# Batch 0's keys in fp32 over the SP queue, pads first, p in three gated loads, refitted load times and a new written order

## The chip, the core and the metric

The kernel runs on one core of one Trainium2 chip. The metric is device time in microseconds (us) of one launch. The engines are TensorE (PE, with its weight loads PEld), VectorE (DVE), ScalarE (ACT), GpSimd (POOL) and SyncE (SP), each of which takes its own list of instructions in order and waits on semaphores for the others. DMAs are issued by SP, by ACT and by POOL; POOL's can change the type on the way (fp32 to bf16), SP's here do not.

## The reference

Inputs: q, k, v of 8 batches x 8 heads x 576 tokens x 64, p of 8 x 8 x 32 x 64, and two weight matrices, 512 x 2048 and 2048 x 512. The output is 4608 x 512, fp32.

```python
p_packed = sm_attn(p, k, v)          # softmax(p k^T / 8) v : 32 packed rows per head
out = sm_attn(q, p_packed, p_packed) # softmax(q p_packed^T / 8) p_packed
x = out.transpose(0, 2, 1, 3).reshape(4608, 512)
y = relu(x @ w_in)**2 @ w_out
```

## The kernel before, in words

Work goes batch by batch (b = 0 to 7), heads in two halves of four (qd = 0, 1). The packed rows are multiplied with w_in first: M = p_packed w_in (32 rows per head, 2048 columns), so that the second softmax's weights, times M, give the hidden layer at once. All PE work is bf16 into fp32 PSUM.

The steps of a batch have names that the kernel's planner uses, and which the text below uses too (lines of the profile in brackets):
- Tk, Tq: DVE transposes of keys and queries (L589, L586). P, PT: cast and transpose of p (L541, L544).
- S1 (PE, L606), MX (DVE row maximum, L609), EX (ACT exp, L612), E (PE transposes, L618), EC (copy out of PSUM by ACT or DVE), PV (PE, L629), RC and XN (DVE, L633, L636): the first softmax and the packed rows. XQ (DVE, L640), XM (PE, L643), XC (copy): two transposed forms of them.
- M.b.0 to 3 (PE, L653), with the casts MC to bf16 on ACT or DVE (L509, L511): packed rows times a quarter of w_in's columns each.
- S2.b.x (PE, L670), then on DVE SI, SM, SU, SS, SN, SO (L683, L686, L690, L696 and L697, L701, L707), with SE (ACT exp, L693) between SU and SS: the second softmax over two parts x of a batch's tokens (three in batch 0). SO writes the weights a2 in the layout that PE needs.
- F1.b.fb (PE, L717; F.b.x.j at L744 for batches 0 and 1, by parts): 128 hidden columns from M and a2. R (relu, L726 and L728; L752 and L754) takes them out of PSUM into one of five buffers r_b, and the square SQ or Q (L734, L736; L762, L764) writes gT and frees the buffer.
- F2.t.fb (PE, L770): 36 tiles t of 128 tokens, 16 matmuls each, gT times w_out. FC copies a tile to one of four o_sb buffers (L509, L511), ST stores it with four DMAs (L785). The last tile is split in two (FZ, L791).

F1.b needs all of SO.b and its quarter of MC.b; F2 tile t needs the squares of the batches that it touches (tiles 9 to 12 lie in batch 2, tile 13 in 2 and 3, tiles 14 to 17 in 3). M and a2 have two buffers, so batch b waits there for F1 of b - 2.

The order of each engine's list is fixed when the program is built. `Plan.forward` (line 70) is a list scheduler: every step has a price per engine, a level (10 b and up) plus an offset from `TABLE['o']`, and where ACT and DVE can both do it, a lean from `TABLE['l']`. At every moment the ready step of the lowest level plus offset is taken. `Plan.run` (line 199) then emits the steps in order of their planned starts. `fills` (line 213) puts dummy matmuls (`keep_clock`, L515) into planned gaps of PE before the first F2. On the chip no planned time is kept, only the order and the semaphores.

Loads are planned as two steps, an issue on POOL (SP for the first half of batch 0's keys) and a stay on "DMA", in the order that the string `ORDER` (line 217) writes: k, v and q of a batch, `x` and `y` the two parts of batch 0's queries, `a0` to `a3` the quarters of w_in (four loads each), `b0` to `b7` eighths of w_out. At most eight POOL loads are under way: the ninth waits for the first to land. `dma_k0` (line 563) brings the first half of batch 0's keys in fp32 to the unused gT over SP, and `k0_cast` (line 567) casts it, part on DVE, part on ACT. `p_load` (line 532) loads p of batch 0 over ACT and p of the other seven batches in one load (448 KB) over SP, held back by a one-element memset (`p_gate`, line 536) until MX.0.1. `setup2` (line 521) zeroes the pads of four v buffers on POOL, four memsets behind the second w_out load.

Of the kernel before, what the change touches and what calls it, by code (L numbers as in the profile page):

```python
# [8 lines left out]
ACT = mybir.ActivationFunctionType  # L9
ALU = mybir.AluOpType  # L10
AX = mybir.AxisListType
F32 = mybir.dt.float32
# [3 lines left out]
D = 64  # L16
# [25 lines left out]
class Plan:  # L42
# [156 lines left out]
    def run(self):  # L199
        out, T = self.forward()  # L200
        free = dict(self.base)
        end = min(p.start for p in out if p.name[:2] == "F2")
        for p in sorted(out, key=lambda p: p.start):
            e, us, fn = p.alts[p.alt]
            if e == "PE" and p.start < end:
                self.keep(self.fills(p.start - free.get(e, 0.0), p.start))
            free[e] = p.end
            u = [[b for b in range(24) if m >> b & 1] for m in p.unit or ()]
            if fn is not None:
                fn(*u)  # L210
        return T

    def fills(self, gap, t):
        return max(0, int((0.9 * gap - 0.3) / (0.2135 if t < self.warm else 0.109))) if gap > 0.7 else 0


ORDER = "k0 v0 x0 a0 y0 a1 a2 a3 b0 b1 k1 b2 b3 v1 b4 q1 b5 b6 b7 k2 v2 q2 k3 v3 q3 k4 v4 q4 k5 v5 q5 k6 v6 q6 k7 v7 q7"

TABLE = {'o': {'Lk.0.0i': 13.26, 'Lk.0.0': -22.5, 'LP.0': 0.67, 'Lk.0.1i': -185.35, 'Lk.0.1': -2.85, 'Lv.0.0i': 94.46,
# [209 lines left out]
def kernel_impl(tc, q, k, v, p, w_in, w_out, out):  # L429
# [24 lines left out]
    with ExitStack() as ctx:  # L454
# [81 lines left out]
        def p_gate():  # L536
            nc.vector.memset(p_f[1][:, :1], 0.0)
# [25 lines left out]
        def dma_k0(slot):  # L563
            kq_of["k", 0, 0] = kq_b[slot]
            nc.sync.dma_start(k0_f, kq_src("k", 0, 0))
# [491 lines left out]
```

## Time and profile before

| | |
|---|---|
| median of 3 runs | 254.42 us (254.21 to 255.92) |
| the profiled execution | 254.59 us, span 252.8 us |
| PE, DVE, ACT, POOL busy | 231.7, 185.0, 146.6, 53.5 us |
| DMA queues: POOL's, SP's | 18.19 MB, 10.30 MB |
| first useful matmul (S1 of batch 0) | 6.24 us |
| S1 of batch 1 | 37.02 us |
| last matmul ends | 247.7 us |

The page gives busy time for each engine, the span in 40 slices (a digit is tenths of busy time, 6.3 us a slice), groups of instructions by line with the mean time of one, and what ended the idle time before them. A stretch's table gives busy time of every engine between two times. A row of the timeline has start, length, engine, line, operation, output and inputs, count, and in brackets idle time with what ended it. PE's ends are modelled: a single F2 matmul is listed with 379 ns, but in a dense row they start 0.21 to 0.22 us apart.

### The profile page before, as it was taken

The numbers are of one execution on the slowest core, as the hardware profiler recorded it, in microseconds if no ns is written. First come the engines' busy times: TensorE is split into PE (matmuls) and PEld (weight loads), VectorE is DVE, ScalarE is ACT, GpSimd is POOL, SyncE is SP. The second block draws the span as 40 slices with busy tenths as digits, with TensorE's granted clock in tenths as the row PEclk, the third lists the DMA queues.
The fourth block names the chain that finished last, engine by engine and source line by source line (L and its number), as shares of the span: only waits on it lengthen the run. The fifth ranks groups of instructions, "written<-read, shape, count | busy, mean of one in ns | idle before, by whom it ended". The sixth has DMA issues, their size and how long they took to land.

```text
span 252.8 us, 5947 instructions
## 1 busy us (share of the span) xinstructions
PE 231.7 (92%) x2364; PEld 131.0 (52%) x2396; DVE 185.0 (73%) x355; ACT 146.6 (58%) x250; POOL 53.5 (21%) x94
## 2 busy tenths in 40 slices
PE   6567898899799999999999999999999999999991
PEld 4344674345454556466453366465544574476451
DVE  3357896898789899866299999967769786956110
ACT  3224795359468669677349589188555591388000
POOL 8559944443334432000000000000000000000001
PEclk9799999999999999999999999999999999999998
DMA  6999999999999999840211210110330311230232
GB/s 151 186 179 172 193 202 207 206 223 244 222 222 205 238 241 210 157 102 2 57 33 40 65 42 23 43 42 3 83 79 19 88 30 40 54 75 0 62 78 70
DMA packets 27147, 29.00 MB, mean 115 GB/s; under 512 B 5776, under 2 KB 18832, under 8 KB 27120
## 3 DMA queue, kind: packets, MB, share of 16 engines
q0 software_dynamic: 17888, 18.19, 43.8%
q1 hardware_dynamic: 8864, 10.30, 15.6%
q8 instruction: 19, 0.31, 0.5%
q10 hardware_dynamic: 368, 0.13, 0.2%
q14 instruction: 8, 0.07, 0.1%
HBM read 37.22 MB, written 9.44 MB: 185 GB/s over the span
## 4 chain that ended last, share of the span: by engine, by line
PE 65%; DMA 17%; DVE 6%; POOL 4%; ACT 2%; issue 2%; SPq 2%; DVEq 0%; POOLq 0%
PE pb L770 36%; PE ps L717 18%; DMA out_dram<-o_sb 4%; DMA kq_b<-in_q_dram 4%; DMA v_b<-in_v_dram 3%; DMA w_in_b<-in_moe_w_in_dram 3%; DMA kq_b<-in_k_dram 3%; PE ps L744 2%; PE ps L653 2%; SPq L785 2%; PE ps L670 2%; PE pb L791 1%; PE ps L770 1%; POOL w_in_b L578 1%; DVE o_sb L511 1%
## 5 line engine op out<-in xcount | busy, mean ns | idle before, releaser
L770 PE MATMUL pb<-w_out_b,gT 128*128 128x512 bf16 x482 | 119.2, 379 | 2.3 <-issue 1.1
L770 PEld LDWEIGHTS <-gT 128*128 128x128 bf16 x560 | 51.8, 98 | 58.5 <-issue 6.2
L717 PE MATMUL ps<-a,M 128*128 128x288 bf16 x384 | 54.9, 286 | 0.2
L726 ACT ACTIVATE r_b<-ps 128x576 bf16<-128x576 f32 x79 | 46.3, 664 | 9.5 <-PE ps L717 9.0
L717 PEld LDWEIGHTS <-M 128*128 128x128 bf16 x384 | 37.4, 98 | 13.5
L736 DVE TENSOR_TENSOR gT<-r_b 128x576 bf16<-128x576 bf16 x73 | 32.9, 455 | 13.7 <-ACT r_b L726 9.6
L785 POOL DMA_DIRECT2D out_dram<-o_sb x2 | 1.1, 532 | 148.6 <-ACT o_sb L509 148.6
L509 ACT COPY o_sb<-pb 128x512 f32<-128x512 f32 (+1 forms) x21 | 11.9, 565 | 32.9 <-PE pb L770 30.7
L509 ACT CAST M<-ps 128x1024 bf16<-128x1024 f32 (+1 forms) x27 | 23.6, 922 | 12.3 <-PE ps L653 9.4
L693 ACT ACTIVATE e<-s 128x512 bf16<-128x512 f32 (+3 forms) x17 | 11.2, 660 | 16.3 <-DVE s L690 16.3
L612 ACT ACTIVATE e<-ps,n 128x576 bf16<-128x576 f32 x16 | 11.8, 738 | 14.3 <-DVE n L609 13.8
L744 PE MATMUL ps<-a,M 128*128 128x256 bf16 (+3 forms) x160 | 18.3, 262 | 1.2 <-DVE a L707 1.2
L609 DVE TENSOR_REDUCE n<-ps 128x1 f32<-128x576 f32 x16 | 11.6, 748 | 7.8 <-PE ps L606 7.7
L744 PEld LDWEIGHTS <-M 128*128 128x128 bf16 x160 | 13.7, 98 | 5.8 <-DVE a L707 1.9
L752 ACT ACTIVATE r_b<-ps 128x512 bf16<-128x512 f32 (+2 forms) x23 | 14.1, 650 | 4.3 <-PE ps L744 3.8
L511 DVE COPY o_sb<-pb 128x512 f32<-128x512 f32 x13 | 8.8, 679 | 10.4 <-PE pb L770 7.2
L734 ACT ACTIVATE gT<-r_b 128x576 bf16<-128x576 bf16 x23 | 14.6, 679 | 0.1
L586 DVE STREAM_TRANSPOSE qT<-kq_b 128x576 f32<-128x576 f32 (+2 forms) x18 | 12.3, 689 | 2.7 <-DMA kq_b<-in_q_dram 2.7
L770 PE MATMUL ps<-w_out_b,gT 128*128 128x512 bf16 x46 | 12.2, 379 | 1.6 <-DVE o_sb L511 0.8
L589 DVE STREAM_TRANSPOSE kT<-kq_b 128x576 f32<-128x576 f32 x16 | 12.0, 754 | 2.2 <-DMA kq_b<-in_k_dram 2.2
L683 DVE STREAM_TRANSPOSE s<-ps 128x512 f32<-128x512 f32 (+3 forms) x17 | 12.1, 731 | 1.9 <-PE ps L670 1.7
L574 POOL DMA_DIRECT2D v_b<-in_v_dram x16 | 11.2, 708 | 9.7 <-DMA kq_b<-in_k_dram 3.6
(63 smaller groups left out, 258.4 us busy)
## 6 DMA issues: line engine op xcount, KB each, us to landing
out_dram<-o_sb SPq DMA_DIRECT2D x138, 64.0 KB, 2.0
kq_b<-in_k_dram POOLq DMA_DIRECT2D x15, 288.0 KB, 10.7
v_b<-in_v_dram POOLq DMA_DIRECT2D x8, 320.0 KB, 10.7
v_b<-in_v_dram POOLq DMA_DIRECT2D x8, 256.0 KB, 9.9
w_in_b<-in_moe_w_in_dram POOLq DMA_DIRECT2D x16, 128.0 KB, 6.6
w_out_b<-in_moe_w_out_dram POOLq DMA_DIRECT2D x8, 256.0 KB, 9.3
kq_b<-in_q_dram POOLq DMA_DIRECT2D x7, 288.0 KB, 11.1
kq_b<-in_q_dram POOLq DMA_DIRECT2D x14, 144.0 KB, 10.2
```

The lines of the kernel that those rows point to most:

```text
L509: nc.scalar.copy(dst, src)
L586: nc.vector.transpose(qT[:, qd].rearrange("p s x -> p (s x)").bitcast(F32)[:, w], kq_of["q", b, qd][:].bitcast(F32)[:, w])
L589: nc.vector.transpose(kT[:, qd].rearrange("p s x -> p (s x)").bitcast(F32).rearrange("p (x a j2) -> p j2 x a", a=32, j2=2), kq_of["k", b, ...
L612: nc.scalar.activation(e1[:, qd], ps1[b, qd], ACT.Exp, bias=n1[b % 2][:, qd:qd + 1], accum_out=d1[b % 2][:, qd:qd + 1])
L683: nc.vector.transpose(flat(s2, b, x).rearrange("p (q n) -> p q n", q=NQD), ps2[b, x])
L717: nc.tensor.matmul(t[:, c], lhsT=M[b % 2][:, qd, fb * FB:(fb + 1) * FB], rhs=a2[b % 2][:, qd, c * HALF:(c + 1) * HALF], start=(qd == 0), s ...
L726: nc.scalar.activation(dst, src, ACT.Relu)
L734: nc.scalar.activation(dst, r, ACT.Square)
L736: eng.tensor_tensor(out=dst, in0=r, in1=r, op=ALU.mult)
L744: nc.tensor.matmul(t[:, c, m * w:(m + 1) * w], lhsT=M[b % 2][:, qd, fb * FB:(fb + 1) * FB], rhs=a2[b % 2][:, qd, o:o + w], start=(qd == 0) ...
L752: nc.scalar.activation(dst, ph["h", b, x, j], ACT.Relu)
L770: nc.tensor.matmul(po[t], lhsT=gT[:, fb, n0:n0 + P], rhs=w_out_b[:, fb, :], start=(fb == 0), stop=(fb == NFB - 1))
```

## The change

1. Both halves of batch 0's keys come in fp32 over SP, into four rows of gT, each with a cast on DVE and one on ACT (`KHW = 2`). POOL no longer issues the second half.
2. The pad memsets of the v buffers go to the head of POOL's list, before the first v load.
3. p comes in three loads: batch 0 over ACT as before, batch 1 (64 KB) over SP behind MX.0.1, batches 2 to 7 (384 KB) over SP behind XQ.1.
4. In `ORDER` the keys of batch 1 move ahead of b0 and b1, its values ahead of b2 and b3, its queries ahead of b4.
5. The planner's load times are changed: 2.0 us after an issue and 0.9 after the stay, with other stays.
6. `fills` counts gap time before `warm` (4.9 us, before 6.6) at 0.2135 us a matmul and the rest at 0.109. The list has 86 dummy matmuls instead of 68.
7. `TABLE` is another one, all offsets and leans (805 and 555 of them). The order of nearly every engine's list changes from the start to the end; the amount of work in the matmuls of the kernel proper does not. DVE has 367 rows in its list instead of 356, ACT 228 instead of 239.

```diff
-                self.keep(self.fills(p.start - free.get(e, 0.0), p.start))
+                self.keep(self.fills(free.get(e, 0.0), p.start))
...
-    def fills(self, gap, t):
-        return max(0, int((0.9 * gap - 0.3) / (0.2135 if t < self.warm else 0.109))) if gap > 0.7 else 0
+    def fills(self, a, b):
+        if b - a < 0.7:
+            return 0
+        cold = max(0.0, min(b, self.warm) - a)
+        return int(cold / 0.2135 + max(0.0, 0.9 * (b - a - cold) - 0.3) / 0.109)
...
-ORDER = "k0 v0 x0 a0 y0 a1 a2 a3 b0 b1 k1 b2 b3 v1 b4 q1 b5 b6 b7 k2 v2 q2 k3 v3 q3 k4 v4 q4 k5 v5 q5 k6 v6 q6 k7 v7 q7"
+ORDER = ("k0 v0 x0 a0 y0 a1 a2 a3 k1 b0 b1 v1 b2 b3 q1 b4 b5 b6 b7 "
+         "k2 v2 q2 k3 v3 q3 k4 v4 q4 k5 v5 q5 k6 v6 q6 k7 v7 q7")
+
+KHW = 2
...
-        p_f = [consts.tile([P, n * D], F32, name=f"p_f{n}") for n in (2, 14)]
+        p_f = [consts.tile([P, n * D], F32, name=f"p_f{i}") for i, n in enumerate((2, 2, 12))]
...
-        def p_gate():
-            nc.vector.memset(p_f[1][:, :1], 0.0)
+        def p_gate(i):
+            nc.vector.memset(p_f[i][:, :1], 0.0)
...
-        k0_f = gT[:, 0:2, :].rearrange("p a b -> p (a b)").bitcast(F32)
+        k0_f = [gT[:, 2 * qd:2 * qd + 2, :].rearrange("p a b -> p (a b)").bitcast(F32) for qd in QDS]
...
-        def dma_k0(slot):
-            kq_of["k", 0, 0] = kq_b[slot]
-            nc.sync.dma_start(k0_f, kq_src("k", 0, 0))
+        def dma_k0(qd):
+            kq_of["k", 0, qd] = kq_b[qd]
+            nc.sync.dma_start(k0_f[qd], kq_src("k", 0, qd))
...
-            add(f"{name}i", [("POOL", issue, fn)], list(deps) + old, line="load", level=-200)
-            add(name, [("DMA", us, None)], [f"{name}i"], line="dma", lag=1.8, level=-200)
+            add(f"{name}i", [("POOL", issue, fn)], list(deps) + old, line="load", lag=2.0, level=-200)
+            add(name, [("DMA", us, None)], [f"{name}i"], line="dma", lag=0.9, level=-200)
...
+        if KHW > 1:
+            add("I2", [("POOL", 2.1, setup2)], line="load", level=-250)
...
-        add("G", [("DVE", 0.06, p_gate)], ["MX.0.1"], level=-99)
-        add("LP.1i", [("SP", 0.5, lambda: p_load(1, 1, B, nc.sync))], ["G"], level=-99)
+        for i, n, gate in ((1, 1, "MX.0.1"), (2, 6, "XQ.1")):
+            add(f"G.{i}", [("DVE", 0.06, lambda i=i: p_gate(i))], [gate], level=-99)
+            add(f"LP.{i}i", [("SP", 0.5, lambda i=i, b0=(0, 1, 2, B)[i], b1=(0, 1, 2, B)[i + 1]: p_load(i, b0, b1, nc.sync))], [f"G.{i}"], lag=1.0, level=-99)
...
-        plan.warm, plan.keep = 6.6, keep_clock
+        plan.warm, plan.keep = 4.9, keep_clock
```

In the changed program's lists, as built, PE goes through F2.7, F2.9, F2.10 and F2.12 before PV.3, and then through S1.4, XM.3, F2.11 with M.3 and S2.3 among it, E.4, S1.5, PV.4, E.5, S1.6, PV.5, XM.5, XM.4, S2.4, E.6, S1.7, PV.6, F1.3 with F2.13 among it, M.4. DVE's list around it reads, in order:

```
FC.12 XN.3 XQ.3 MX.4.1 Tk.5.0 MC.3.0 MX.4.0 Tk.5.1 SI.3.0 SM.3.0 SI.3.1 EC.4.0 SM.3.1 EC.4.1
Tk.6.0 SU.3.1 Tk.6.1 MX.5.0 SS.3.1 MX.5.1 SN.3.1 SU.3.0 SO.3.1 Tq.4.0 MX.6.0 MX.6.1 SS.3.0
Tk.7.0 Tk.7.1 Tq.4.1 SN.3.0 RC.5 SO.3.0 XN.5 RC.4 XQ.5 XN.4 XC.5 XQ.4 XC.4 SI.4.0 RC.6 Tq.5.0
SI.4.1 MX.7.0 SM.4.1 MX.7.1 Tq.5.1 EC.7.0 RC.7 SQ.3.0 EC.7.1 SQ.3.1 SQ.3.2 SU.4.1 ...
```

More of the change, by code (lines that the diff above doesn't have):

```diff
@@ L211, in run @@
         return T
-    def fills(self, gap, t):
-        return max(0, int((0.9 * gap - 0.3) / (0.2135 if t < self.warm else 0.109))) if gap > 0.7 else 0
-ORDER = "k0 v0 x0 a0 y0 a1 a2 a3 b0 b1 k1 b2 b3 v1 b4 q1 b5 b6 b7 k2 v2 q2 k3 v3 q3 k4 v4 q4 k5 v5 q5 k6 v6 q6 k7 v7 q7"
-TABLE = {'o': {'Lk.0.0i': 13.26, 'Lk.0.0': -22.5, 'LP.0': 0.67, 'Lk.0.1i': -185.35, 'Lk.0.1': -2.85, 'Lv.0.0i': 94.46,
[207 rows of a table removed]
+    def fills(self, a, b):
[6 more added lines that the diff above has]
+KHW = 2
+TABLE = {'o': {'Lk.0.0i': 114.0, 'Lk.0.1i': -41.03, 'Lk.0.0': 7.9, 'LP.0': 105.76, 'Lk.0.1': -41.22, 'I2': 113.03,
[207 rows of a table added]
 def kernel_impl(tc, q, k, v, p, w_in, w_out, out):
@@ L558, in dma_kq, with k0_cast @@
                 nc.gpsimd.dma_start(t[64 * g:64 * g + 64, w], kq_src(nm, b, qd)[64 - 64 * g:128 - 64 * g, w])
-        k0_f = gT[:, 0:2, :].rearrange("p a b -> p (a b)").bitcast(F32)
+        k0_f = [gT[:, 2 * qd:2 * qd + 2, :].rearrange("p a b -> p (a b)").bitcast(F32) for qd in QDS]
         K0 = 10 * D
-        def dma_k0(slot):
-            kq_of["k", 0, 0] = kq_b[slot]
-            nc.sync.dma_start(k0_f, kq_src("k", 0, 0))
-        def k0_cast(i, eng):
+        def dma_k0(qd):
+            kq_of["k", 0, qd] = kq_b[qd]
+            nc.sync.dma_start(k0_f[qd], kq_src("k", 0, qd))
+        def k0_cast(qd, i, eng):
             w = slice(0, K0) if i == 0 else slice(K0, JT * D)
-            cast(eng, kq_of["k", 0, 0][:, w], k0_f[:, w])
+            cast(eng, kq_of["k", 0, qd][:, w], k0_f[qd][:, w])
         def dma_v(b, i):
@@ L816, in load @@
             old = [issued[-8]] if len(issued) >= 8 else []
-            add(f"{name}i", [("POOL", issue, fn)], list(deps) + old, line="load", level=-200)
-            add(name, [("DMA", us, None)], [f"{name}i"], line="dma", lag=1.8, level=-200)
+            add(f"{name}i", [("POOL", issue, fn)], list(deps) + old, line="load", lag=2.0, level=-200)
+            add(name, [("DMA", us, None)], [f"{name}i"], line="dma", lag=0.9, level=-200)
             issued.append(name)
-        add("Lk.0.0i", [("SP", 0.45, lambda: dma_k0(0))], level=-300)
-        add("Lk.0.0", [("DMA", 1.36, None)], ["Lk.0.0i"], line="dma", lag=1.7, level=-300)
-        add("LP.0", [("DMA", 0.25, None)], line="dma", lag=1.7, level=-299)
+        for qd in range(KHW):
+            add(f"Lk.0.{qd}i", [("SP", 0.4, lambda qd=qd: dma_k0(qd))], lag=0.8, line="SPk", level=-300)
+        if KHW:
+            add("Lk.0.0", [("DMA", 2.0, None)], ["Lk.0.0i"], line="dma", lag=0.55, level=-300)
+        add("LP.0", [("DMA", 0.25, None)], line="dma", lag=0.8, level=-299)
+        if KHW > 1:
+            add("Lk.0.1", [("DMA", 1.8, None)], ["Lk.0.1i"], line="dma", lag=0.6, level=-300)
+        if KHW > 1:
+            add("I2", [("POOL", 2.1, setup2)], line="load", level=-250)
         for x in ORDER.split():
@@ L838, in kernel_impl @@
                     kq_free[slot] = f"T{nm}.{n}.{qd}" + (".y" if y else "")
-                    if x == "k0" and qd == 0:
+                    if x == "k0" and qd < KHW:
                         continue
                     for g in (0, 1) if nm == "q" and qd == 1 else (None,):
-                        load(f"L{nm}.{n}.{qd}{y}" + ("" if g is None else f".{g}"), (js[1] - js[0]) * 0.0755 * (1 if g is None else 0.5),
+                        load(f"L{nm}.{n}.{qd}{y}" + ("" if g is None else f".{g}"), (js[1] - js[0]) * 0.088 * (1 if g is None else 0.5),
                              lambda nm=nm, n=n, qd=qd, slot=slot, g=g, js=js: dma_kq(nm, n, qd, slot, g, js), 0.56, old)
@@ L845, in kernel_impl @@
                 for i in range(2):
-                    load(f"Lv.{n}.{i}", 1.33 + 0.3 * i, lambda n=n, i=i: dma_v(n, i), 0.7, [f"PV.{n - NV}"] if n >= NV else [])
+                    load(f"Lv.{n}.{i}", 1.15 + 0.55 * i, lambda n=n, i=i: dma_v(n, i), 0.7, [f"PV.{n - NV}"] if n >= NV else [])
             elif x[0] == "a":
@@ L849, in kernel_impl @@
                     for qd in QDS:
-                        load(f"LWI.{n}.{i}.{qd}", 0.62, lambda n=n, i=i, qd=qd: dma_w_in(n, i, qd), 0.6)
+                        load(f"LWI.{n}.{i}.{qd}", 0.665, lambda n=n, i=i, qd=qd: dma_w_in(n, i, qd), 0.6)
             else:
-                load(f"LWO.{n}", 1.26, lambda n=n: dma_w_out(n), 0.73)
-        add("G", [("DVE", 0.06, p_gate)], ["MX.0.1"], level=-99)
-        add("LP.1i", [("SP", 0.5, lambda: p_load(1, 1, B, nc.sync))], ["G"], level=-99)
-        add("LP.1", [("DMA", 1.0, None)], ["LP.1i"], lag=2.0, level=-99)
-        for i, (b0, b1) in ((0, (0, 1)), (1, (1, B))):
+                load(f"LWO.{n}", 1.42, lambda n=n: dma_w_out(n), 0.73)
+        for i, n, gate in ((1, 1, "MX.0.1"), (2, 6, "XQ.1")):
+            add(f"G.{i}", [("DVE", 0.06, lambda i=i: p_gate(i))], [gate], level=-99)
+            add(f"LP.{i}i", [("SP", 0.5, lambda i=i, b0=(0, 1, 2, B)[i], b1=(0, 1, 2, B)[i + 1]: p_load(i, b0, b1, nc.sync))], [f"G.{i}"], lag=1.0, level=-99)
+            add(f"LP.{i}", [("DMA", 0.32 * n, None)], [f"LP.{i}i"], lag=0.9, level=-99)
+        for i, (b0, b1) in enumerate(((0, 1), (1, 2), (2, B))):
             add(f"P.{i}", [("DVE", 0.07 + (b1 - b0) * 0.066, lambda i=i, b0=b0, b1=b1: p_cast(i, b0, b1))], [f"LP.{i}"], level=-9)
             add(f"PT.{i}", [("DVE", 0.07 + (b1 - b0) * 0.066, lambda b0=b0, b1=b1: p_tr(b0, b1))], [f"P.{i}"], level=-9)
-        add("KC.0", [("DVE", 0.42, lambda: k0_cast(0, V))], ["Lk.0.0"], level=-10)
-        add("KC.1", [("ACT", 0.48, lambda: k0_cast(1, A))], ["Lk.0.0"], level=-10)
+        for qd in range(KHW):
+            add(f"KC.{qd}.0", [("DVE", 0.4, lambda qd=qd: k0_cast(qd, 0, V))], [f"Lk.0.{qd}"], level=-10)
+            add(f"KC.{qd}.1", [("ACT", 0.5, lambda qd=qd: k0_cast(qd, 1, A))], [f"Lk.0.{qd}"], level=-10)
         def lasts(b):
@@ L885, in kernel_impl @@
                 add(f"Tk.{b}.{qd}", [("DVE", 0.69, lambda b=b, qd=qd: tr_k(b, qd))],
-                    ([f"Lk.{b}.{qd}"] if b or qd else ["KC.0", "KC.1"]) + ([f"S1.{b - 1}" if b > 1 else f"S1.0.{qd}"] if b else []), line="Tk", level=L)
-            pt = f"PT.{min(b, 1)}"
+                    ([f"Lk.{b}.{qd}"] if b or qd >= KHW else [f"KC.{qd}.0", f"KC.{qd}.1"]) + ([f"S1.{b - 1}" if b > 1 else f"S1.0.{qd}"] if b else []), line="Tk", level=L)
+            pt = f"PT.{min(b, 2)}"
             if b in SOLO:
@@ L983, in kernel_impl @@
                     add(f"ST.{t}", [("SP", 2.45, lambda t=t: store(t))], [f"FC.{t}"], free=[(f"FC.{t}", 0)], lag=2.0, level=L)
-                    add(f"SD.{t}", [("DMA", 0.5, None)], [f"ST.{t}"], level=L)
+                    add(f"SD.{t}", [("DMA", 0.42, None)], [f"ST.{t}"], level=L)
                 else:
@@ L1002, in kernel_impl @@
         add("I", [("POOL", 0.7, lambda: masks.make_identity(nc, ident[:]))], ["Lv.0.1i"], level=-250)
-        add("I2", [("POOL", 2.1, setup2)], ["LWO.1i"], level=-250)
+        if KHW < 2:
+            add("I2", [("POOL", 2.1, setup2)], ["LWO.1i"], level=-250)
         p_load(0, 0, 1, nc.scalar)
         setup()
-        plan.base.update(DVE=1.4, POOL=1.2, ACT=2.1, SP=0.7, DMA=1.2, PE=1.1)
+        plan.base.update(DVE=1.4, POOL=1.2, ACT=2.1, SP=0.7, DMA=1.6, PE=1.1)
         plan.table = TABLE
-        plan.warm, plan.keep = 6.6, keep_clock
+        plan.warm, plan.keep = 4.9, keep_clock
         kernel_impl.plan = plan
```

414 rows, old and new, of the table TABLE are left out of this document.

## The prediction

> **What bounds the kernel now.** I read the page's busy shares, then its 40 slices, then the busy table of chosen stretches, then the DVE groups by shape, and last the timeline of PE around batch 3. All of it is one execution: span 252.8 us, 254.59 us in all, so 1.8 us lie outside the span; the median of three runs is 254.42.
>
> ```profile
> span 252.8 us, 5947 instructions
> PE 231.7 (92%) x2364; PEld 131.0 (52%) x2396; DVE 185.0 (73%) x355; ACT 146.6 (58%) x250; POOL 53.5 (21%) x94
> ...
> PE   6567898899799999999999999999999999999991
> ...
> DVE  3357896898789899866299999967769786956110
> ```
>
> TensorE is full from slice 6 on. What can move is the start (0 to 31 us), any hole torn into the rest, and the 5.1 us after the last matmul.
>
> ```profile
> 37.02:108.94 71.92, 67.76 (x750) 36.15 (x761) 62.12 (x114) 46.90 (x80) 26.00 (x44) 1.00 1.16 214
> ...
> 108.94:247.72 138.78, 136.85 (x1289) 76.33 (x1307) 99.11 (x188) 81.47 (x137) 0.87 (x2) 1.00 0.19 47
> ```
>
> Columns: stretch, length, busy PE, PEld, DVE, ACT, POOL, granted clock, DMA. 37.02 is batch 1's S1, 108.94 batch 3's first F1 chunk. PE is nearly seamless because DVE, with as much as 62 of 72 us of work, is spread beside it. At 88.94 comes PV.3, at 108.94 F1.3.0: in those 20 us DVE makes batch 3's weights (SO.3) while PE runs F1.2 and F2 tiles.
>
> ```profile
> 88.94 0.48 PE L629 MATMUL ps<-v_b,e1T 128*32 128x64 bf16 x40 [0.33 <-ACT r_b L726]
> ...
> 108.94 1.27 PE L717 MATMUL ps<-a,M 128*128 128x288 bf16 x9
> ```
>
> The price list of DVE:
>
> ```profile
> L736 DVE TENSOR_TENSOR gT<-r_b 128x576 bf16<-128x576 bf16 x73 | 32.9, 455 | 13.7 <-ACT r_b L726 9.6
> L589 DVE STREAM_TRANSPOSE kT<-kq_b 128x576 f32<-128x576 f32 x16 | 12.0, 754 | 2.2 <-DMA kq_b<-in_k_dram 2.2
> ...
> L609 DVE TENSOR_REDUCE n<-ps 128x1 f32<-128x576 f32 x16 | 11.6, 748 | 7.8 <-PE ps L606 7.7
> L586 DVE STREAM_TRANSPOSE qT<-kq_b 128x576 f32<-128x576 f32 x14 | 10.4, 751 | 0.8 <-DMA kq_b<-in_q_dram 0.8
> ...
> L511 DVE CAST M<-ps 128x1024 bf16<-128x1024 f32 x7 | 8.4, 1203 | 2.4 <-PE ps L653 2.4
> ```
>
> Over all shapes count times mean is 202.4 us, the busy time 185.0: neighbours overlap by 17.4/355 = 0.05 us, which I take off each. For PE I use start-to-start times of dense timeline stretches: F2 0.217 us, F1 0.49 a chunk, M 0.26, S1 0.65, E 0.28, PV 0.45, an S2 half 0.36, XM 0.23.
>
> **The start.** Key half k0.1 leaves POOL's queue for SP's, in fp32. Removed: one POOL issue (0.68) and a landing at 8.4. SP's fp32 half k0.0 was issued at 0.75 and used at 4.62; behind it, at about 300 GB/s (the 2 to 4 us windows), the second lands near 6.6. Added: a cast on DVE (0.49, the row of the first half) and on ACT (0.62), both on the path: S1.0.1 starts about 8.9 instead of 9.21. The pads, 1.96 us of POOL at 25.26, go to the head: the first v load issues at 1.95 + 1.96 - 0.68 = 3.23. Cover: the second fp32 half keeps the DMA rings busy until then; without cover it costs 1.28.
>
> ```profile
> 8.00:9.00 1.00, 0.00 (x0) 0.00 (x0) 0.62 (x1) 0.00 (x0) 0.36 (x1) 0.91 1.39 201
> 9.00:10.00 1.00, 0.79 (x8) 0.30 (x11) 0.80 (x2) 0.16 (x1) 0.60 (x2) 0.50 1.36 190
> ```
>
> The clock fell to 0.50 after PE stood idle from 6.93 to 9.21, and S1.0.1 took 1.15 us, S1.0.0 0.69. Twelve new fills stand in that gap: 0.46 back there, about 0.3 in E.0.0. p's 448 KB, in flight from 11.2 to 18.9 beside query and w_in loads, become 64 KB; 384 KB move past 40 us. At the windows' 190 GB/s that is 2.0 us of stream, less about 0.4 for the wider key half, so w_in's third chunk, whose wait ended last (PE until 26.38), lands about 1.6 earlier. Two small p steps (0.17, 0.15) join DVE. Walking M.0.3 and the F pieces on, S1.1 starts near 32.9 with 11.1 us of useful matmul done; before, that much was done at 37.0 - 2.8 = 34.2. **Start: -1.3**, between +1.3 (pads uncovered, nothing else) and -3.0 (all p bytes and all cold clock).
>
> **Up to PV.3.** k1, v1, q1 move up by two, two and one w_out loads (1.4 us each by the landings that POOL waits on); q1's last half, awaited at 44.78, comes near 42. But between S2.1 and SO.1.1 DVE now also has the large p cast and transpose (0.48 + 0.50) and Tk.2.0, whose key lands about 50.5. SP's queue: the last p load stands ahead of all stores, its gate opens near 42, the first store came at 50.76: no wait. From S1.1 to F1.3.0 before, 67.0 us of listed matmul took 71.9, 5.0 lost; I leave 5.0 (bounds 2 and 8). The changed PE list has 67.8 us from S1.1 through PV.3: it ends at 32.9 + 67.8 + 5.0 = 105.7.
>
> **The new order around batch 3** decides. PE's list now runs F2.7, 9, 10 and 12 in a row (11 us from F2.7.13 on) *before* PV.3; DVE then has only copies, because the next thing in its list, XN.3, needs PV.3. After it, DVE's list is:
> - XN.3 to SO.3.0: 32 pieces, 20.7 us. Only 9.9 are batch 3's; 10.8 are keys, maxima, queries and copies of batches 4 to 7.
> - XN.5 to SO.4.0: 44 pieces, 23.0 us. Eight of F1.3's squares (3.2) stand among 19.7 of batches 4 to 7.
> - SQ.3.8 to SQ.3.15: 14 pieces, 7.9 us, with both MC.4 casts that F1.4.0 needs.
>
> That is 51.5 us in series. PE's list beside it, S1.4 to F2.13.15, holds 27.5 us, of which F2.11 and F2.13 are all the filler there is: F2.14 to F2.17 need F1.3, F1.3.0 needs SO.3.0, each later F1.3 chunk a relu slot (5) freed by those squares, F2.13.15 needs SQ.3.15. Walked piece by piece with ACT's steps, from PV.3's end: SO.3.0 +21.0; then XM.4, S2.4, E.6, S1.7, PV.6 stand in PE's queue; F1.3.0 +25.8, F1.3.3 +34.3, SO.4.0 +44.7, F2.13.15 +52.9. **Starved: 52.9 - 27.5 = +25.4**; bounds 15 (the 30.5 us of batches 4 to 7 a third cheaper than their rows) and 30 (F1.3 on one PSUM pair throughout, 1.3 us a chunk from +34.3).
>
> **The clock in it.** The walk leaves PE idle from +8.9 to +12.2 and +16.3 to +21.3, longer than the 2.3 us after which the clock halved; fills stop at the first F2. At half clock the 15.3 us of PE from F1.3.0 on need 30.6 where the walk gives 27.1: **+3** (bounds 0, all under DVE, and 8, with the first part's chain doubled too).
>
> The Trainium skill (TensorE: Matmul & The Clock Gate, What's actually happening) puts both changes at about 3.4 us, idle to throttle and busy to release; this trace throttled after 2.3, but released after about 3 (9.2 to 12.2), which agrees. By the page's idle figure only the second gap would throttle, and this term would be about 1, the total 280.
>
> **The rest.** S2.6.0 to the end is 111.6 us of listed matmul; before, 137.2 listed took 138.8, so 113. F1.5 has relu on DVE alone: two relus and a square, 1.8 us, against 1.63 of PE, six pairs, +1. Against before: +0.7.
>
> **Sum.** 105.7 + 52.9 + 3 + 113 + 1 = 275.6; after the last matmul 5.1; outside the span 1.8: 282.5, **282 us**. As differences: 254.6 - 1.3 + 25.4 + 3 + 0.7 = 282.4.
>
> **Rivals.**
> - *A smaller hole.* DVE's pieces are cheaper with little beside them: hole at 15, 2 instead of 5 lost before PV.3, no clock term: 254.6 - 1.3 - 3 + 15 + 0.7 = 266. For it: the means come from a busy trace. Against it: the same rows are as long in its quiet stretches (a key transpose took 0.72 to 0.78 everywhere).
> - *Half clock to the end of F1.3 and beyond*: clock term 8, hole 30: 292. For it: sparse PE at +8.9 to +34. Against it: dense PE releases it within 3 us.
> - *Not slower.* The hole is covered: front pieces of batches 4 to 7 run while PE has F2, so that 51.5 shrinks to PE's 27.5. Place: SO.3.0 before F1.3.0. Price: 254.6 - 1.3 + 0.7 = 254.0, or 252.3 at the start's bound. It decides only if DVE's 51.5 comes under 30. Against it: both engines take their lists in order, and XN.3 heads that list.
>
> **How the numbers follow.** Forecast 0.63 (own range 272 to 290), smaller hole 0.20, half clock 0.10, not slower 0.07. Range 263 to 293, leaving out the last case, the low edge of the second and the high one of the third. 1% (2.5 us) is about what a measurement of this kernel can tell: faster 0.03, same 0.04, slower 0.93.
>
> **What would show it.** Right: PE slices of 3 to 6 tenths from about 106 to 160 us with DVE at 9, PE waiting for L713 (SO) and L742 or L734 pieces, clock below 1 in that stretch; F1.3.0 some 26 us behind PV.3; clock 1.0 at 8 to 12 us; S1.1 near 33. Wrong: a full PE row there, or DVE idle inside the hole, which would make another engine or a store its cause.

## The result, and the profile after

After: 291.8 us (median; 289.9 to 293.7), before beside it 254.3. The ratio is 1.147, with a 95% interval of 1.136 to 1.158. The profiled execution took 290.9 us, span 289.1. The forecast was 282 us, range 263 to 293. Of the runs below, some executions were slower at a lower granted clock; the ratios leave those out.

The page of the changed kernel: the busy shares, and three rows of the 40 slices (7.2 us each, numbered from 1, tenths busy; the last row is the granted clock).

```profile
span 289.1 us, 6036 instructions
PE 251.6 (87%) x2414; PEld 138.2 (48%) x2414; DVE 189.1 (65%) x367; ACT 145.6 (50%) x243; POOL 52.4 (18%) x93
...
PE   8777889669888999944676979999999999999994
...
DVE  3569888479597860799798999958928115534300
...
PEclk9979999968999999995585999999999999999999
```

PE's busy time rose too, from 231.7 to 251.6 us, although its work is the same but for 18 dummy matmuls. Part of that is matmuls at a lower clock, and part is missing records: the trace before has 2364 matmuls beside 2396 weight loads, this one 2414 of both. The row has two dents where the row before was full: a small one at slices 8 and 9 (51 to 65 us), with the clock down to 6, and the large one at slices 18 to 24 (123 to 173 us), with the clock down to 5. In the large one DVE is at 7 to 9 tenths; in slice 16, ahead of PV.3, DVE is at 0. The stretches between the prediction's own landmarks (busy PE, PEld, DVE, ACT, POOL, clock, DMA): from batch 1's S1 to the end of PV.3, from there to batch 6's first S2, from there to the last matmul.

```profile
33.91:117.22 83.31, 73.72 (x716) 39.00 (x715) 57.82 (x106) 44.35 (x74) 25.36 (x43) 0.96 1.04 190
117.22:171.60 54.38, 38.14 (x599) 20.00 (x591) 50.52 (x99) 28.10 (x50) 1.05 (x2) 0.78 0.08 18
171.60:284.87 113.27, 113.07 (x785) 60.88 (x784) 59.10 (x112) 56.44 (x91) 0.79 (x2) 1.00 0.21 51
```

The second is the foreseen hole: PE busy for 38.1 of 54.4 us, DVE for 50.5. The third is as seamless as before. The first is the surprise: 83.3 us where the forecast had 72.8. PE's timeline says where most of that went:

```profile
53.30 2.75 PE L776 MATMUL pb<-w_out_b,gT 128*128 128x512 bf16 x12
59.47 0.41 PE L612 MATMUL ps<-kT,pT 32*32 32x512 bf16 x4 [3.41 <-DVE pT L550]
```

Batch 2's S1 waited 3.41 us for PT.2. DVE's timeline shows why, and the list of DMA issues how long the load took (KB, then us from issue to landing):

```profile
57.62 0.56 DVE L547 TENSOR_SCALAR p_b<-p_f 128x768 bf16<-128x768 f32 x1 [3.64 <-DMA p_f<-in_p_dram]
```
```profile
p_f<-in_p_dram SPq DMA_DIRECT2D x1, 384.0 KB, 15.0
```

P.2 stood 3.64 us for p's third load, issued at 42.6 and landed 15.0 us later; SN.1.1 and SO.1.1 stood behind it on DVE. The granted clock was 0.66 from 60 to 70 us.

In the hole, DVE's first line shows the idle time ahead of PV.3, and PE's lines its waits for DVE and ACT behind it:

```profile
116.96 0.69 DVE L517 COPY o_sb<-pb 128x512 f32<-128x512 f32 x1 [11.05 <-PE pb L776]
```
```profile
129.73 0.71 PE L624 MATMUL ps<-ident,e 128*128 128x128 bf16 x5 [3.17 <-ACT e L618]
...
138.79 0.29 PE L649 MATMUL ps<-ident,pp 128*128 128x128 bf16 x1 [3.53 <-DVE pp L642]
...
152.63 0.95 PE L723 MATMUL ps<-a,M 128*128 128x288 bf16 x4 [2.76 <-DVE s L689]
```

### The profile page after: what moved, and what is told of

The parts are those of the page before. It is cut to its first block, busy times and chain, and to the rows that moved or that the text cites. A ratio compares the mean times of both kernels' runs of the same rounds, so it can differ in the third digit from the quotient of the medians.

```text
span 289.1 us, 6036 instructions
## 1 busy us (share of the span) xinstructions
PE 251.6 (87%) x2414; PEld 138.2 (48%) x2414; DVE 189.1 (65%) x367; ACT 145.6 (50%) x243; POOL 52.4 (18%) x93
## 3 DMA queue, kind: packets, MB, share of 16 engines
q0 software_dynamic: 17744, 17.90, 37.8%
## 4 chain that ended last, share of the span: by engine, by line
PE 58%; DMA 23%; DVE 8%; ACT 5%; issue 3%; POOL 2%; SPq 1%; ACTq 0%; DVEq 0%; POOLq 0%
PE pb L776 33%; PE ps L723 16%; DMA v_b<-in_v_dram 6%; DMA w_in_b<-in_moe_w_in_dram 4%; DMA kq_b<-in_q_dram 4%; DMA kq_b<-in_k_dram 4%; DMA w_out_b<-in_moe_w_out_dram 3%; DMA out_dram<-o_sb 2%; PE ps L659 2%; ACT r_b L732 1%; PE ps L776 1%; PE ps L750 1%; PE ps L612 1%; PE pb L797 1%; PE ps L676 1%
## 5 line engine op out<-in xcount | busy, mean ns | idle before, releaser
L776 PE MATMUL pb<-w_out_b,gT 128*128 128x512 bf16 x512 | 127.2, 381 | 1.4 <-DVE o_sb L517 1.2
L723 PE MATMUL ps<-a,M 128*128 128x288 bf16 x384 | 60.2, 293 | 5.5 <-DVE s L689 2.8
L723 PEld LDWEIGHTS <-M 128*128 128x128 bf16 x384 | 38.1, 100 | 26.4 <-issue 8.3
L732 ACT ACTIVATE r_b<-ps 128x576 bf16<-128x576 f32 x67 | 41.1, 652 | 18.2 <-PE ps L723 17.4
L750 PE MATMUL ps<-a,M 128*128 128x256 bf16 (+3 forms) x160 | 21.6, 281 | 4.5 <-ACT r_b L758 1.5
L734 DVE TENSOR_SCALAR r_b<-ps 128x576 bf16<-128x576 f32 x29 | 20.3, 747 | 6.5 <-PE ps L723 6.5
L564 POOL DMA_DIRECT2D kq_b<-in_q_dram x18 | 9.5, 533 | 43.7 <-DVE qT L592 36.9
L517 DVE COPY o_sb<-pb 128x512 f32<-128x512 f32 (+1 forms) x8 | 5.3, 658 | 17.2 <-PE pb L776 15.1
L521 PE MATMUL pb<-zero 128*128 128x256 bf16 x86 | 14.6, 336 | 1.1 <-DVE zero L524 1.1
L659 PE MATMUL ps<-w_in_b,ppT 64*32 64x512 bf16 x256 | 12.0, 391 | 3.3 <-DVE ppT L517 2.6
L517 DVE CAST M<-ps 128x1024 bf16<-128x1024 f32 (+1 forms) x9 | 9.8, 1097 | 7.4 <-PE ps L659 7.0
```

The costliest lines, as they stand in the source:

```text
L517: eng.tensor_copy(dst, src)
L521: nc.tensor.matmul(half(7)[:, :2 * P], lhsT=zero[:, :P], rhs=zero, start=True, stop=True)
L659: nc.tensor.matmul(half(u[qd])[o:o + 32], lhsT=ppT[b % 2][r, w:w + 32], rhs=w_in_b[r, h, c * WCH:(c + 1) * WCH], start=True, stop=True)
L723: nc.tensor.matmul(t[:, c], lhsT=M[b % 2][:, qd, fb * FB:(fb + 1) * FB], rhs=a2[b % 2][:, qd, c * HALF:(c + 1) * HALF], start=(qd == 0), s ...
L732: nc.scalar.activation(dst, src, ACT.Relu)
L734: nc.vector.tensor_scalar_max(dst, src, 0.0)
```

## The experiments

Where an edit must not disturb the order, I had the planner's result written out (piece, engine, PSUM halves, dummy matmuls ahead of it), changed in that list what is named, and let the kernel emit it. Times are medians, ratios against the kernel before beside them (253.1 to 253.4 us).

### Order without loads, loads without order

```diff
-        out, T = self.forward()
+        for x in SEQ.split():
+            name, alt, units, nf = x.split(":")
...
```

> The kernel before, with all its loads as they were (one fp32 key half over SP, p in two loads, pads late), but every engine's list put by hand into the order of the kernel after. Theory (the order of the lists around batch 3 costs nearly all): the hole of 54 us from PV.3 to F2.13.15 stays, the 3.41 us wait for the last p load and the slow clock behind it go, the start's gain goes too: 286 us (280 to 291), F1.3.0 some 27 us behind PV.3. Rival (the new loads cost most of the 37 us): at most 265.

> The other half: the loads of the kernel after (two fp32 key halves over SP, pads first, p in three gated loads, its order of loads on POOL) under the lists of the kernel before; P.2 and PT.2 stand behind batch 1's second SS on DVE. Theory (the order costs nearly all): 255 us (252 to 259): the start's 1 to 2 us gained, a wait of up to 4 us for the last p load, no hole around batch 3. Rival (the loads cost most): above 265.

Order alone: 287.5 us, ratio 1.136 [1.132, 1.140]. Loads alone: 259.9, ratio 1.027 [1.023, 1.031]. So the order costs about 34 us and the loads 6.5 by themselves. The first theory held for the order. The loads' 259.9 us lie just above the 259 that its range allowed, and well below the rival's 265. Batch 1's S1 came at 38.4 us with the new loads, where the profile before has 37.0; PE waited 2.35 us for w_out at 30.3, k1, v1 and q1 now being ahead of most w_out loads.

The stretch from PV.3 to F1.4's first wait for an M copy took 53.3 us with the new loads (the kernel after) and 53.3 with the old; here with the old, under the order of after:

```profile
112.51:165.81 53.30, 37.05 (x622) 19.60 (x621) 49.31 (x95) 26.86 (x48) 1.05 (x2) 0.78 0.09 18
```

The larger part of the loads' loss is a second kind of wait. PE, DVE and SP of the kernel with the loads alone (SP's line: total us waited, times, longest):

```profile
65.92 1.01 PE L750 MATMUL ps<-a,M 128*128 128x256 bf16 x4 [4.38 <-DVE r_b L760]
```
```profile
63.39 0.69 DVE L517 COPY o_sb<-pb 128x512 f32<-128x512 f32 x1 [4.76 <-DMA out_dram<-o_sb]
```
```profile
SPq L791 <- DMA p_f<-in_p_dram: 5.0, 1, 5.0
```

Here P.2 came late enough for its load. But SP stood 5.0 us at a *store* until p had landed; output buffers ran out, a copy on DVE waited 4.76 us for one, and PE behind it 4.38.

### The same load from ACT's queue

```diff
-... p_load(i, b0, b1, nc.sync) ...
+... p_load(i, b0, b1, nc.sync if i == 1 else nc.scalar) ...
```

> The loads of after under the lists of before, as in the run that took 259.9 us, but p's last load issued from ACT's queue instead of SP's. There PE stood idle for 4.38 us near 62 us behind a copy on DVE that waited for an output store. Theory (the stores wait on SP's queue behind p's 384 KB): the idle goes, 255.5 us (254 to 257.5). Rival (the load's own landing, or its bytes, hold the work up): 258.5 or more.

265.0 us, ratio 1.045 [1.037, 1.053]: the rival's side, and slower still. (A part lies ahead of this place: batch 1's S1 came at 40.0 us in this profile, 38.4 in the one with SP.) SP now waited longer for a load that was no longer in its queue:

```profile
SPq L791 <- DMA p_f<-in_p_dram: 6.3, 1, 6.3
```
```profile
75.33 0.69 DVE L517 COPY o_sb<-ps 128x512 f32<-128x512 f32 x1 [6.79 <-DMA out_dram<-o_sb]
```

The waits in the program explain it. The DMAs of SP and ACT signal eight completion counters in turn, and most stores wait for the DMA that used their counter last, eight earlier. In this program p's load on ACT's queue has the fifth counter. The next seven DMAs, all stores on SP, have the others; the eighth is a store that waits for the fifth. The profile agrees: p landed 16.8 us after its issue at 47.4, and that store was issued at 64.1. In the run before it, with p on SP, the eighth DMA behind p's load is again the store that waits: the load was issued at 45.7 and took 15.8 us, the store followed at 61.5.

A load that takes so long thus blocks the eighth DMA behind it, whichever of the two queues it was issued from. The first theory's word "queue" was wrong; what the store waits for is the landing.

### p's last load earlier

```diff
-        for i, n, gate in ((1, 1, "MX.0.1"), (2, 6, "XQ.1")):
+        for i, n, gate in ((1, 1, "MX.0.1"), (2, 6, "SO.0.2")):
```

> The kernel after, every list as it is, but the gate and the issue of p's last load (384 KB) behind batch 0's last SO instead of behind batch 1's XQ: issued near 28 us, needed at 54. Theory (what the forecast missed between S1.1 and PV.3 is the wait for that load and the slow clock behind it): no idle ahead of batch 2's S1, clock 1.0 in 60 to 70 us, PV.3 at 109 to 112 instead of 116.8, 286 us (283 to 288). Rival (its bytes then hold up the key, value and w_out loads of 30 to 45 us as much): 289 or more.

285.2 us, ratio 1.128 [1.123, 1.132]: 6.6 less than after by the medians, about 5 by the ratios (the interval of after's ratio alone is some 3 us to either side). That is what the theory had. PV.3 came at 110.9, batch 2's S1 went without a wait, and the clock was 1.00 from S1.1 to PV.3:

```profile
53.17 2.75 PE L776 MATMUL pb<-w_out_b,gT 128*128 128x512 bf16 x12
55.86 1.03 PE L612 MATMUL ps<-kT,pT 32*32 32x512 bf16 x32
```
```profile
33.73:111.31 77.58, 71.29 (x715) 37.53 (x715) 57.52 (x105) 43.99 (x74) 25.44 (x43) 1.00 1.11 203
```

The load did not become faster: it took 16.1 us here. It was only issued early enough to land before P.2.

### The filler behind PV.3, and ahead of it

```diff
+        for x in plan.pieces:
+            if x.name in ("F2.9.0", "F2.10.0", "F2.12.0"):
+                x.deps.append("PV.3")
```

> The kernel after with one rule more for its planner: F2.9, F2.10 and F2.12 may not start before PV.3; all up to that place is as in the kernel after. Theory (the hole comes from putting the filler ahead of PV.3, so that DVE idles before and PE behind): PV.3 some 11 us earlier, those F2 tiles run under batch 3's softmax, the starved time falls from 27 to 8 to 13 us: 275 us (270 to 281). Rival (DVE's list from XN.3 on is too long wherever PV.3 stands): within 3 us of the 291.8 of after.

274.8 us, ratio 1.082 [1.076, 1.088]: 17 us less. From PV.3 to F1.3.0 took 24.0 us here, 27.4 in the kernel after, and PE had work for most of it:

```profile
104.55:128.56 24.01, 21.58 (x350) 9.47 (x349) 22.43 (x39) 12.13 (x18) 1.05 (x2) 1.00 0.27 61
```
```profile
116.80:144.18 27.38, 17.64 (x434) 9.11 (x434) 24.61 (x47) 12.40 (x23) 1.05 (x2) 0.72 0.16 34
```

The first line is this kernel, the second the kernel after. The rule is not the only difference, though: the planner, given the rule, builds another order for everything behind that place. DVE's list now has 37 pieces from XN.3 to SO.3.0 (32 in after), and 18 from there to SO.4.0 (44 in after). The 17 us are the worth of the rule with all that the planner makes of it.

The converse, in the kernel before with its own loads:

```diff
+        for x in plan.pieces:
+            if x.name == "PV.3":
+                x.deps.append("F2.12.15")
```

> The kernel before, loads and all, with one rule more for its planner: PV.3 may not start before F2.12's last matmul, so that F2.9, F2.11 and F2.12 run ahead of it. Theory (that alone tears the hole): 254.6 plus 22 to 30 us, 280 us (275 to 286), DVE idle ahead of PV.3 and PE at 3 to 6 tenths behind it. Rival (the hole needs the new loads or the slow clock of the first part): below 262.

283.3 us, ratio 1.118 [1.114, 1.122]. One rule to the planner makes a tuned kernel 30 us slower, and its rows (slices of 7.0 us) have the same shape: DVE at 6 and 0 tenths in slices 14 and 15, ahead of PV.3 at 110.6 us, PE down to 3 tenths in slices 17 to 21, behind it. F1.3.0 came 36.9 us behind PV.3.

```profile
PE   6569999998999997753458899999999999999993
...
DVE  2459978997898608699998799983660445252010
```

Here too the planner changed more than the place of PV.3: DVE's list from XN.3 to the last SO.3 grew from 31 pieces to 58, most of the new ones front pieces of batches 4 to 7. So the two runs show that the rule costs or saves that much together with the order that follows from it. How much is the filler ahead of PV.3, and how much the pieces that then stand between XN.3 and SO.3, they do not tell apart.

### DVE's share of the hole, and the clock's

```diff
         def tr_q(b, qd, js=(0, JT)):
+            if b in (5, 6):
+                return
...
         def tr_k(b, qd):
+            if b in (5, 6, 7):
+                return
```

> The kernel after without ten of DVE's transposes, the keys of batches 5, 6 and 7 and the queries of batches 5 and 6 (these batches are then computed from old keys and queries). All ten stand in DVE's list between XN.3 and F1.3's last square. Theory (that list, in series, sets the hole's length): 10 times 0.70 us less, the hole 47 instead of 54 us, 284 us (281 to 287). Rival (the hole is a chain through PE and ACT, DVE has room): 289 or more.

Ratio 1.133 [1.125, 1.140], which is 287 us, the upper end of the theory's range. Only two executions stand behind it, and the profiled one is not among them, so that I rest the verdict on the next pair.

```diff
-        def keep_clock(n):
+        def keep_clock(n, u=7):
...
```

> The kernel after with dummy matmuls (108 in all, 256 columns each) put ahead of the nine places in the hole where PE stood idle, into PSUM halves that are free there. Theory (DVE sets the hole, the halved clock costs only where PE was on the path): clock near 1.0 from 126 to 160 us and 1 to 3 us less, 289 to 291. Rival (the halved clock makes much of the hole): 285 or less. Other rival (the dummies stand in the way): 292 or more.

> The kernel after with both edits in the hole: the ten transposes of batches 5 to 7 left out, and the 108 dummy matmuls. Alone each took about 3 us off the 53.3 from PV.3 to F1.4's first chunk (50.8 and 50.2). Theory (DVE's list in series, once PE runs at full clock): the cut shows in full, 43 to 45 us from PV.3 to F1.4.0. Rival (PE, ACT and DVE pass batch 3's and the next batches' steps to each other in one chain, each waiting for the other): 47 to 48 us.

With dummies 289.9 us, ratio 1.145 [1.137, 1.154]; with both edits 288.5, ratio 1.139 [1.133, 1.145]. These totals hardly differ from after's. In the profiled executions one reason is seen: batch 1's S1 came at 36.4 and 35.1 us, where after had 33.9, by landings of the first loads that the edits don't touch (P.1 waited 4.27 and 3.82 us for p's second load, 2.50 in after). The stretch from PV.3 to F1.4's wait for M can be compared; in order the kernel after, with dummies, with dummies and the cut:

```profile
116.80:170.08 53.28, 37.10 (x621) 19.60 (x621) 49.30 (x95) 26.91 (x48) 1.05 (x2) 0.78 0.09 19
```
```profile
120.72:170.96 50.24, 43.32 (x730) 26.84 (x730) 48.66 (x95) 27.11 (x48) 1.05 (x2) 1.00 0.09 20
```
```profile
119.82:167.66 47.84, 42.92 (x730) 26.94 (x730) 43.04 (x85) 26.98 (x48) 1.05 (x2) 1.00 0.10 20
```

The dummies raise the clock from 0.78 to 1.00 and take 3.0 us off: this is the clock term. (Three executions with this order and no dummies took 53.3, 53.3 and 53.7 us.) Split at F1.3.0, in the same order, first the kernel after and then the one with dummies:

```profile
144.18:170.08 25.90, 19.46 (x195) 10.50 (x188) 24.68 (x49) 14.51 (x25) 0.00 (x0) 0.83 0.01 2
...
120.72:146.20 25.48, 22.04 (x501) 13.69 (x500) 24.06 (x47) 12.52 (x23) 1.05 (x2) 1.00 0.18 37
146.20:170.96 24.76, 21.28 (x241) 13.15 (x231) 24.60 (x49) 14.59 (x25) 0.00 (x0) 1.00 0.01 2
```

Ahead of F1.3.0 the dummies save 1.9 us (27.4, the line shown above, against 25.5), behind it 1.1.

At full clock DVE is busy for 48.7 of 50.2 us, so its list does set the pace. But 5.6 us less of DVE shorten the stretch by only 2.4; DVE's idle time grows from 1.6 to 4.8, and by the timeline it is spent in waits for PE (3.0) and ACT (1.0). The rival (47 to 48 us) held: close behind DVE stands a chain through PE and ACT. A small part of that chain is the dummies' own: XM.5 started at 139.66, when 30 of them were through, though its input was ready at 139.16.

### Both repairs, and the start alone

> The kernel after with the two repairs together: the three F2 tiles held until PV.3 (274.8 us alone) and p's last load gated at batch 0's last SO (285.2 alone, 6.6 less than after). Theory (two separate losses, the second ahead of the first in time): they add, 268.3 us (266 to 271). Rival (the wait for p is swallowed by the hole that is left): 273 or more.

268.9 us, ratio 1.061 [1.057, 1.066]. The two losses add: 17.0 and 6.6 by themselves, 22.9 together. Some 16 us against the kernel before remain; the order differs in many places, and I did not take them apart. The largest dent that is left in PE's row lies around F1.3.0, which waits 1.51 us for SO.3: from 120 to 130 us PE is busy for 6.1 of 10.

```diff
+        for qd in range(KHW):
+            add(f"Lk.0.{qd}i", [("SP", 0.4, lambda qd=qd: dma_k0(qd))], lag=0.8, line="SPk", level=-300)
...
+            add("I2", [("POOL", 2.1, setup2)], line="load", level=-250)
```

> The lists, the order of loads and p's two bytes-early loads (all of p issued near 10 us) of the kernel before, with only two parts of the change: both fp32 halves of batch 0's keys over SP with their casts, and the pads first on POOL (and five dummy matmuls ahead of the second S1). Theory (the start alone gains, since nothing else is touched): second S1 near 7.5 instead of 9.2 us, S1.1 0.5 to 2 us earlier, 252.3 us (251 to 253.5) against 253.4. Rival (the first loads are given back at the w_in and w_out waits near 26 to 30 us): 253.4 or more.

> As the run beside it, but p in three loads, the last (384 KB) gated at batch 0's last SO (near 28 us) instead of behind batch 1's XQ. Theory (p's last load costs only by when it lands, and by the stores that wait for it; at 28 us it does neither): 252.3 us (251 to 253.5), not the 259.9 that the gate behind XQ took under the same lists. Rival (384 KB among the w_out, key and value loads of 28 to 45 us costs what it saves): 254.5 or more.

252.9 us, ratio 0.999 [0.996, 1.002], and 254.4, ratio 1.006 [1.002, 1.009]. Neither beats the kernel before. Both have the load order of before. The first, PE's timeline:

```profile
7.63 0.69 PE L612 MATMUL ps<-kT,pT 32*32 32x512 bf16 x16 [0.21 <-DVE kT L595]
...
18.75 0.26 PE L676 MATMUL ps<-qT,pq 32*32 32x192 bf16 x4 [2.85 <-DVE qT L592]
```

Batch 0's second S1 is 1.6 us earlier and at full clock; then batch 0's second S2 waits 2.85 us for a query transpose (1.23 before). That transpose waits for its load and starts only 0.4 us earlier than before (18.06 against 18.42); batch 1's S1 is 0.3 us earlier (36.69). In the second kernel S1.1 came at 34.1 instead of 37.0, but a w_out wait of 2.07 us at 40.8 and a 0.77 us wait for pT followed. The median of the first lies inside the theory's range, but the ratio leaves at most 1 us of the gain. So the rivals' reason held, a gain that is given back at a later load; the place that the first rival named, the weight loads near 26 to 30 us, did not, and neither time reached the figure that its rival gave.

## Why the prediction was right, and where it was not

The forecast's case came: slower, by the hole around batch 3. Its parts, against the profiled execution (forecast 282.4, measured 290.9; the median, 291.8, lies inside the whole range but above the forecast's own, 272 to 290):

| step | forecast | measured | difference |
|---|---|---|---|
| S1.1 starts | 32.9 | 33.9 | +1.0 |
| S1.1 to the end of PV.3 | 72.8 | 83.3 | +10.5 |
| hole, to S2.6.0 (52.9 and clock 3) | 55.9 | 54.4 | -1.5 |
| S2.6.0 to the last matmul | 114 | 113.3 | -0.7 |
| behind it, and outside the span | 6.9 | 6.0 | -0.9 |

- **The new order** was right in place, cause and size. From the end of PV.3: SO.3.0 at +21.4 (forecast 21.0), F1.3.0 +27.0 (25.8), F1.3.3 +35.4 (34.3), SO.4.0 +46.5 (44.7). The order alone cost 34 us. The signs that the prediction named came in part: DVE was idle for only 3.9 of the 54.4 us, F1.3.0 and S1.1 came near their places, and the clock was 1.00 from 8 to 12 us. The waits that it named for PE did not: F1.3.0 had none for SO (L713), and PE's longest waits in the hole were for an exponential of ACT (3.17 us), pp (3.53) and s (2.76).
- **"51.5 us in series" on DVE** was right as a length, too strong as a cause: cut by 5.6 at full clock, the stretch gave 2.4. The walk could hit all the same, because the chain through PE and ACT is nearly as long.
- **The clock**, +3: measured 3.0, the right size in part by luck. The walk's two gaps came, at +9.3 to +12.5 us and +18.0 to +21.6 (forecast +8.9 to +12.2 and +16.3 to +21.3). But the prediction put the whole term behind F1.3.0, where 1.1 us of it were found; 1.9 lay ahead, where it had put nothing. The gap before 129.73 was 3.17 us, the clock in it fell to 0.50 about 2.4 us after PE's last matmul, and batch 6's S1 after it ran at half clock (1.15 us for 28 matmuls; 0.70 is usual for 32). The Trainium skill (TensorE: Matmul & The Clock Gate, What's actually happening) asks for about 3.4 us of idle window; it also says that the window runs freely. The forecast's variant by that figure, a term of 1, did not hold.
- **Up to PV.3** is the step that failed. "The large p cast and transpose (0.48 + 0.50)" priced the work and not the wait for its load, and "SP's queue ... no wait" held for the gate but not for the landing, 15.0 us. With the load earlier the stretch fell from 83.3 to 77.6, so 5.7 of the 10.5. The rest, 4.8, is the term "67.8 us of listed matmul, 5.0 lost": without the p wait PE was busy for 71.3 us of this stretch and idle for 6.3, so 3.5 is more busy time than the list's 67.8 and 1.3 more idle time than the 5.0. Why the list came out longer, at a clock of 1.00, was not taken apart.
- **The start**, -1.3: the sign is not shown. With the lists of after, S1.1 came anywhere from 31.7 to 36.4 us in the six profiled executions that can be compared; P.1, priced at 0.17, waited 2.50 us for p's second load in after and 0.53 in the kernel with the filler held. Alone, the start's change gave 0.999 [0.996, 1.002]: what it gains is given back at a later load.
- **The rivals.** The smaller hole (266) and the covered one (254) did not come; with three tiles held back, and the order that the planner then makes, 17 us of it went, a step toward what the "not slower" rival would have needed. The time fell beside the 292 of the half-clock rival, but not by its mechanism: the hole was no longer than forecast, the clock term was 3.0 and not 8, and the clock was back at 1.00 from 160 us on.

## What to carry to other kernels

A step that opens a long chain on another engine, as PV.3 does here, can need filler behind it. Before moving filler ahead of such a step, add up what each engine's list holds between it and the first work that needs its result. When a rule is given to a planner, compare everything behind the rule's place too, since the planner orders that anew. Price a load by its landing in the traffic in which it will be issued, and look for the DMA that must wait for it, which can be an unrelated store. Follow a gain at the start to the next load that the engine waits for before it is counted.

## What the hardware showed that I had not expected

p's last load moved 384 KB in 15.0 us, 26 GB/s, while the core moved 205 GB/s (42.6 to 57.6 us). In the kernel before, 448 KB near 11 us had taken 7.7 us. The size is not what matters: near 10 us, 384 KB took 8.9 us (the first of the two start kernels) and 448 KB 6.9 (the order alone); issued at 28 us or later, 384 KB took from 13.8 to 16.8 in every run that has this load.

Its packets are small. With the load on ACT's queue that queue had 1920 packets and 0.52 MB, without it 368 and 0.13, which is 0.25 KB a packet; POOL's queue has 17744 packets for 17.9 MB, 1.0 KB each. The Trainium skill (DMA: Bandwidth & Descriptors, Queues, rings and completion order) says that an engine takes turns between queues, and drains a whole packet of one, typically 9 to 17 descriptors, before it goes to the next. Whether the packets that the profile counts are those is not shown. If they were, p would get a fifth by equal turns, about 41 GB/s in the late window and 35 in the early one, as an estimate. Measured were 26 of 205 late and 60 of 177 early, so the trace follows equal turns in neither, and why the late load is slower stays open.
